# Attention in portions, the second output projection after the last down projection, and a residual added by the stores

## The chip, the cores and the metric

One core of a Trainium2 chip runs the whole program in one launch. The metric is the device time of one execution in microseconds (us). TensorE (PE) multiplies matrices, and PEld are its weight loads. VectorE (DVE) does elementwise work, ScalarE (ACT) copies and activations; GpSimd (POOL) and SyncE (SP) mainly issue DMAs here. Every engine, and every queue of DMA issues, works in its written order: an instruction that waits holds up what is written behind it.

## The reference

The input x has 2048 rows (tokens) of 1024 values, in bf16. What is computed:

```
xn  = layernorm(x)
q, k, v = xn @ wqkv                    # wqkv 1024 x 3072, 32 heads of 32
logits[s, w] = q[s] . k[s - 2 w] / sqrt(32),   w = 0..7, masked below row 0
s   = (softmax over w of logits, times v[s - 2 w], summed over w) @ wo
h   = silu(xn @ w1) * (xn @ w3)        # w1, w3 1024 x 3584
out = x + s * silu(h @ w2)             # w2 3584 x 1024
```

The attention is local and dilated: a token sees eight tokens, itself and every second one before it.

## The kernel before

**Products.** Each large matrix product is done in blocks by a scheme of seven products instead of eight (Strassen's, in Winograd's form). One call of `seven` makes the seven products of one block; each product is eight matmuls of 128x512, in groups named by PSUM tiles (`am`, `em`, `bm` in the MLP, `aq`, `eq`, `bq` in qkv). The operands that are sums of weight quarters are made by VectorE (`qkv_sums`, `w_sums`, `w2_step`), those of the output by adds that read PSUM (`um`, `pk`, `h_sb`) and by copies of ScalarE (`act_copy`, L158) from one PSUM tile to the next, for which TensorE waits. PSUM has four tiles of two banks. The last of the seven products is put off into the next block (`pend`, `flush`).

**Stages, in TensorE's order.** The tokens are handled in two halves b of 1024.

- layernorm and qkv: twelve sevens over q, k, v, two halves, two groups g of heads. Results of the first 512 tokens stay in SBUF; those of the other three quarters are written to DRAM through tiles `pk` (`park`, L334, issued by ScalarE).
- `mlp_up(0)`: 14 blocks `fb` of w1 and w3. In this half VectorE also makes the sums of the weights and of w2 and GpSimd stores them (`s_dram`, `t_dram`), so that the second half only loads them.
- `mlp_down(0)`: seven products of 56 matmuls each, then `wo(0)`: seven products of 16.
- `mlp_up(1)`, `wo(1)`, `mlp_down(1)`, whose `gated` multiplies by the attention's projection, adds x (loaded as `xr`) and stores.

**Attention** is on VectorE, in four chunks c of 512 tokens. `scores(c)` makes, for each of the eight w, one product of 128x4096 and three adds (L405 to L408). `score_sums(c)` sums over the 32 values of a head with eight matmuls on TensorE (tile `zp`, weights `ones`, 128x32 each, to four column strips; L416). `softmax(c)` follows, GpSimd spreads the result out (`Ep`, 16 DMAs a chunk), and `values(c)` makes eight products and eight adds or so of 128x4096 (L444, L456, L457). k, v and q of the next chunk come by `fetch_k` and `fetch_v` on GpSimd's queue.

**Order.** A scheduler places each instruction by priority and the order in which the code is written. Work under `hp()` (high priority) comes first; attention is written under `priority(BG ...)`, far behind, and so fills what the other work leaves. `att_step()` releases the next part of it at seven fixed places. `behind(key)` puts an instruction after a named earlier one (`tc.issue_after`).

**Memory for weights.** `wring` has ten slots; `r4` takes a slot and `release` gives it back. SyncE loads, two blocks ahead. Attention has four tiles (`att`, tag `a8`), small results four more (`kk`, tag `k4`).

Of the kernel before, what the change touches and what calls it, by code (L numbers as in the profile page):

```python
# [17 lines left out]
def kernel(  # L18
# [161 lines left out]
    def seven(key, A, B, e11, e12, e22, e21, snap=None):  # L180
# [21 lines left out]
        act_copy(su2[:], pb[:])  # L202
        for i in I:
            mm(pe[:, i], s4[i], b22, False)
# [3 lines left out]
        e22(pb, sp5)  # L208

# [119 lines left out]
    def park(t, c, j0, name):  # L329
        tl = k4(name, (2, CH), BF16)  # L330
        dst = (q_dram, k_dram, v_dram)[t][c, :, j0:j0 + 2, :]

        def fin():
            m = nc.scalar.dma_start(out=dst, in_=tl[:])  # L334
            if spill:
                d, f = spill.pop(0)
                with tc.issue_after(m.ins):
                    nc.scalar.dma_start(out=d, in_=f)

        return tl[:], fin  # L340
# [6 lines left out]
    def qkv_copy(t, c, j0):  # L347
        def f(ps, *a):
            d, fin = qkv_dst(t, c, j0)
            with hp():  # L350
                if a:
                    nc.vector.tensor_add(d, ps[:], a[0][:])
                else:
                    anchor["c", t, c, j0] = nc.scalar.copy(out=d, in_=ps[:])  # L354
                fin()
        return f
# [29 lines left out]

    def fetch_k(c):
        if c == 0:
            return
        nc.gpsimd.tensor_copy(out=kT[:, :, 0:HALO], in_=kT[:, :, CH:CH + HALO])  # L390
        nc.gpsimd.dma_start(out=kT[:, :, HALO:], in_=k_dram[c])
# [3 lines left out]
    def fetch_v(c):  # L395
        nc.gpsimd.tensor_copy(out=vT[:, :, 0:HALO], in_=vT[:, :, CH:CH + HALO])
        nc.gpsimd.dma_start(out=vT[:, :, HALO:], in_=v_dram[c])

    def scores(c):
        q = qt[c]  # L400
        E = att_tile((W, CH), BF16, f"Es{c}")
        for w in range(W):
            o = HALO - DIL * w
            p_t = att_tile((NJ, CH), BF16, f"pt{c}_{w}")
            nc.vector.tensor_mul(p_t[:], q[:], kT[:, :, o:o + CH])  # L405
            nc.vector.tensor_add(p_t[:, 0:4, :], p_t[:, 0:4, :], p_t[:, 4:8, :])  # L406
            nc.vector.tensor_add(p_t[:, 0:2, :], p_t[:, 0:2, :], p_t[:, 2:4, :])
            nc.vector.tensor_add(E[:, w, :], p_t[:, 0, :], p_t[:, 1, :])  # L408
        sc[c] = E

    def score_sums(c):
        E = sc[c]
        zp = bank2(f"zp{c}")
        for h in range(2):
            for sq in range(4):
                nc.tensor.matmul(  # L416
                    zp[sq * 32:(sq + 1) * 32, h].rearrange("p (w t) -> p w t", t=P), lhsT=ones4[:],
                    rhs=E[:, h * 4:(h + 1) * 4, sq * P:(sq + 1) * P], start=True, stop=True,
                )
        sc[c] = E[:].bitcast(FP32).rearrange("p w n -> p (w n)").rearrange("p (a w t) -> p a w t", a=2, t=P)  # L420
        nc.scalar.copy(out=sc[c][:, 0], in_=zp[:].rearrange("p h (w t) -> p (h w) t", t=P))

    def softmax(c):
        Z = sc[c]
        z, zm, zs = Z[:, 0], Z[:, 1, 0:4], Z[:, 1, 4:8]
# [4 lines left out]
        nc.scalar.activation(out=z, in_=z, func=ACTF.Exp, scale=scale)  # L430
# [8 lines left out]
    def values(c, pairs=(0, 2, 4, 6)):  # L439
        E = pr[c]  # L440

        def pvmul(dst, w):
            o = HALO - DIL * w
            nc.vector.tensor_mul(dst, E[:, w, :].unsqueeze(1).to_broadcast([P, NJ, CH]), vT[:, :, o:o + CH])  # L444

        A = oT[:, c % 2]
        for w0 in pairs:
            B = att_tile((NJ, CH), BF16, f"B{c}_{w0}")
            if w0 == 0:
                pvmul(A, 0)  # L450
                pvmul(B[:], 1)
            else:
                C = att_tile((NJ, CH), BF16, f"C{c}_{w0}")
                pvmul(B[:], w0)
                pvmul(C[:], w0 + 1)
                nc.vector.tensor_add(B[:], B[:], C[:])  # L456
            nc.vector.tensor_add(A, A, B[:])  # L457

    def att_steps():
        with priority(BG - 10000):  # L460
            scores(0)
        yield
        score_sums(0)
        fetch_k(1)
        with priority(BG):
            softmax(0)
            scores(1)
            values(0)
            fetch_v(1)
        yield  # L470
        with priority(BG + 9000):
            fetch_k(2)
        yield
        score_sums(1)
        with priority(BG + 10000):
            softmax(1)
            scores(2)
            values(1)
            fetch_k(3)
            fetch_v(2)  # L480
        yield
        score_sums(2)
        with priority(BG + 20000):
            softmax(2)
        yield
        with priority(BG + 30000), behind("wo"):
            scores(3)
            values(2, (0, 2, 4))
        yield
        score_sums(3)  # L490
        with priority(BG + 40000):
            softmax(3)
            values(2, (6,))
            fetch_v(3)
            values(3)
        yield

    att_it = att_steps()

    def att_step():  # L500
        next(att_it)
# [17 lines left out]
    def up_load(b, fb):  # L519
# [7 lines left out]
        else:  # L527
            up_sums(b, fb, w1t, w3t)
            sa, s4 = tiles[b, fb][2:]
            nc.sync.dma_start(out=sa[:], in_=s_dram[fb, :, 0:2])  # L530
            nc.sync.dma_start(out=s4[:], in_=s_dram[fb, :, 3])
# [3 lines left out]
    def up_sums(b, fb, w1t, w3t):  # L535
        sa = r4(("sa", fb), (2, KH, 2 * P), FP16)
        half.append(half.pop(0))
        s4 = slot(5, (KH, 2 * P), FP16, half[0] * SLOT // 2)
        tiles[b, fb] = w1t, w3t, sa, s4

    def w_sums(fb):
        up_sums(0, fb, *tiles[0, fb])
# [3 lines left out]
        with behind(("m", fb - 1)):  # L546
            nc.vector.tensor_add(sa[:, 0], a21, a22)
            nc.vector.tensor_sub(sa[:, 1], sa[:, 0], a11)
            nc.vector.tensor_sub(s4[:], a12, sa[:, 1])
            nc.vector.tensor_sub(s3, a11, a21)  # L550
# [11 lines left out]
    def mlp_up(b, steps={}):  # L562
        order = [*range(b * FB // 2, FB - 1), *range(b * FB // 2), FB - 1]
        for n, fb in enumerate(order):
            steps.get(n, lambda: None)()
            if n == 0:
                up_load(b, fb)
                if b == 0:
                    w_sums(fb)
                up_load(b, order[1])  # L570
# [8 lines left out]
            def e12(pe, su2):  # L579
# [5 lines left out]
                if b == 0:  # L585
                    anchor["m", fb] = m
                    if fb + 1 < FB:
                        w_sums(fb + 1)
                if n + 2 < FB:
                    up_load(b, order[n + 2])  # L590

            def e22(pb, sp5):
                with hp():
                    m = nc.vector.tensor_add(h_sb[:, f2, CH:], pb[:], sp5[:])  # L594
                if b == 0:
                    anchor["t", fb] = m
                    w2_step(fb)

            def e21(pb, f2=f2, hl=hl, n=n, fb=fb):
                release(("w3", fb))  # L600
                with hp():
                    nc.scalar.copy(out=hl["g"][:, :, 0:CH], in_=pb[:])  # L602
                    nc.vector.tensor_mul(h_sb[:, f2, :], h_sb[:, f2, :], hl["g"][:])  # L603

# [372 lines left out]
```

## Time and profile before

| what | value |
|---|---|
| median of 8 runs | 753.09 us (751.89 to 755.47) |
| the profiled execution | 755.47 us, its span 753.8 us |
| granted TensorE clock, mean | 0.989 |
| PE busy | 724.6 us (96%), 3314 instructions |
| PEld busy | 346.5 us (46%) |
| DVE busy | 619.9 us (82%), 602 instructions |
| ACT busy | 312.8 us (41%) |
| POOL busy | 95.6 us (13%) |
| DMA | 153.68 MB, mean 204 GB/s |
| first product of `first_two` starts | 12.46 us |
| `mlp_up(0)` starts | 169.24 us |
| `mlp_down(0)` starts | 349.70 us |
| `wo(0)` starts | 437.64 us |
| `mlp_up(1)` starts | 461.81 us |
| `wo(1)` starts | 636.70 us |
| `mlp_down(1)` starts | 663.62 us |

A row of the profile names an engine, a line of the kernel, an operation and its output and input tiles; "idle before" is how long the engine had stood still, and the name behind the arrow is what ended that. L148 is the helper `mm`, so TensorE's rows are told apart by the tile names. Matmul ends are modelled: a busy TensorE is not one at its peak, and the distance from start to start of two groups is the safer measure.

### The profile page before, as it was taken

To read this page: it belongs to the slowest core of one execution; us is meant where nothing else is said; L and a number is where in the kernel's file an instruction comes from. 1 tells how busy PE (TensorE), PEld (TensorE's weight loads), DVE (VectorE), ACT (ScalarE), POOL (GpSimd) and SP (SyncE) were. 2 spreads that over 40 slices of the span, in tenths; PEclk is the share of its full clock that TensorE was granted. 3 is DMA by queue.
4 is the path that set the end of the run, shared out by engine and by line. 5 is a ranking of instruction groups with operands and counts; after the bars stand their busy time and mean duration, and the time that the engine had idled before them with its cause. 6 is when DMAs were issued, how large, how long until landed. Compare 5 with 4: busy or idle time off the path is not lost.

```text
span 753.8 us, 8738 instructions
## 1 busy us (share of the span) xinstructions
PE 724.6 (96%) x3314; PEld 346.5 (46%) x3367; DVE 619.9 (82%) x602; ACT 312.8 (41%) x327; POOL 95.6 (13%) x156
## 2 busy tenths in 40 slices
PE   8999999899999999989899999999999999999997
PEld 4655565454444444434344444443444444444443
DVE  8988996879999999999899558999984999552143
ACT  5653345335444555443021443443565454420121
POOL 0000001310212253411001402000032000000000
PEclk9999999899999999999999999999999999999999
DMA  9385449844778799979575989554367543624631
GB/s 332 122 164 178 140 153 311 262 139 165 232 242 268 271 308 297 314 249 333 188 231 180 356 232 287 159 164 128 120 185 230 153 134 118 210 89 135 208 114 56
DMA packets 130218, 153.68 MB, mean 204 GB/s; under 512 B 14976, under 2 KB 100480, under 8 KB 129536
## 3 DMA queue, kind: packets, MB, share of 16 engines
q1 hardware_dynamic: 112960, 102.25, 44.4%
q0 software_dynamic: 11024, 37.76, 14.5%
q10 hardware_dynamic: 6192, 13.11, 4.7%
q8 instruction: 26, 0.43, 0.2%
q14 instruction: 16, 0.13, 0.1%
HBM read 107.48 MB, written 39.32 MB: 195 GB/s over the span
## 4 chain that ended last, share of the span: by engine, by line
PE 48%; DVE 38%; issue 7%; DMA 4%; ACT 2%; SPq 0%; DVEq 0%; ACTq 0%
PE db L148 10%; PE de L148 6%; PE bm L148 6%; DVE pt L405 6%; PE bq L148 5%; PE da L148 5%; PE am L148 4%; PE em L148 3%; DVE pt L406 3%; DVE h_sb L594 3%; PE aq L148 3%; DVE um L581 3%; PE eq L148 2%; DVE B L444 2%; DVE h_sb L603 2%
## 5 line engine op out<-in xcount | busy, mean ns | idle before, releaser
L148 PEld LDWEIGHTS <-wring 128*128 128x128 f16 (+1 forms) x1952 | 205.3, 106 | 233.2 <-issue 21.6
L148 PE MATMUL bm<-xs,wring 128*128 128x512 f16 x672 | 156.8, 380 | 7.4 <-DVE h_sb L594 7.2
L148 PEld LDWEIGHTS <-h_sb 128*128 128x128 f16 (+1 forms) x976 | 103.0, 106 | 120.9 <-issue 12.2
L148 PE MATMUL am<-xT,wring 128*128 128x512 bf16 x424 | 105.6, 382 | 3.1 <-ACT bm L158 1.9
L405 DVE TENSOR_TENSOR pt<-qt,kT 128x4096 bf16<-128x4096 bf16 x32 | 73.1, 2288 | 1.0 <-ACT kT L354 0.5
L148 PE MATMUL db<-wring,h_sb 128*128 128x512 f16 x336 | 73.3, 379 | 0.0
L583 ACT ACTIVATE g<-um 128x1024 bf16<-128x1024 f32 x28 | 29.6, 1057 | 86.3 <-DVE um L581 82.5
L148 PE MATMUL em<-xs,wring 128*128 128x512 f16 x224 | 52.9, 379 | 0.0
L148 PE MATMUL em<-xT,wring 128*128 128x512 bf16 x219 | 52.7, 379 | 0.3
L437 POOL DMA_DIRECT2D Ep<-pb x64 | 36.9, 584 | 125.3 <-DVE pb L433 120.8
L148 PE MATMUL da<-wring,h_sb 128*128 128x512 bf16 x220 | 50.5, 388 | 2.2 <-DMA wring<-in_B_w_dram 2.0
L603 DVE TENSOR_TENSOR h_sb<-h_sb,g 128x2048 bf16<-128x2048 bf16 x28 | 34.1, 1219 | 8.0 <-ACT g L602 8.0
L406 DVE TENSOR_TENSOR pt<-pt 128x2048 bf16<-128x2048 bf16 x32 | 39.0, 1220 | 0.4
L577 ACT ACTIVATE h_sb<-am 128x1024 bf16<-128x1024 f32 x28 | 28.6, 1023 | 21.2 <-PE am L148 21.1
L158 ACT COPY pm<-em 128x1024 f32<-128x1024 f32 x28 | 28.3, 1012 | 21.2 <-PE em L148 21.1
L581 DVE TENSOR_TENSOR um<-em,um 128x1024 f32<-128x1024 f32 x28 | 34.1, 1218 | 3.2 <-PE em L148 3.2
L457 DVE TENSOR_TENSOR oT<-oT,B 128x4096 bf16<-128x4096 bf16 x16 | 36.6, 2285 | 0.1
L158 ACT COPY um<-bm 128x1024 f32<-128x1024 f32 x28 | 28.4, 1014 | 19.9 <-PE bm L148 19.9
L444 DVE TENSOR_TENSOR B<-Ep,vT 128x4096 bf16<-128x4096 bf16 x16 | 36.5, 2284 | 0.0
L602 ACT CAST g<-bm 128x1024 bf16<-128x1024 f32 x28 | 28.3, 1011 | 16.3 <-PE bm L148 15.4
L594 DVE TENSOR_TENSOR h_sb<-bm,pm 128x1024 bf16<-128x1024 f32 x28 | 34.1, 1216 | 0.4 <-PE bm L148 0.4
L158 ACT COPY bm<-am 128x1024 f32<-128x1024 f32 x28 | 28.1, 1002 | 9.9 <-PE am L148 9.8
(180 smaller groups left out, 887.3 us busy)
## 6 DMA issues: line engine op xcount, KB each, us to landing
wring<-in_B_w_dram SPq DMA_DIRECT2D x68, 512.0 KB, 5.4
wring<-t_dram SPq DMA_DIRECT2D x16, 512.0 KB, 4.5
s_dram<-wring POOLq DMA_DIRECT2D x14, 512.0 KB, 3.8
s_dram<-wring POOLq DMA_DIRECT2D x28, 256.0 KB, 5.1
t_dram<-wring POOLq DMA_DIRECT2D x14, 512.0 KB, 6.6
wring<-s_dram SPq DMA_DIRECT2D x28, 256.0 KB, 3.0
wring<-s_dram SPq DMA_DIRECT2D x14, 512.0 KB, 3.7
wring<-in_A_wqkv_dram SPq DMA_DIRECT2D x6, 1024.0 KB, 7.0
```

Of the source, the lines that this page charges most:

```text
L148: nc.tensor.matmul(ps, lhsT=lhs[k], rhs=rhs[k], start=(first and k == 0), stop=(k == n - 1), skip_group_check=not first,)
L158: nc.scalar.copy(out=out_, in_=in_)
L405: nc.vector.tensor_mul(p_t[:], q[:], kT[:, :, o:o + CH])
L406: nc.vector.tensor_add(p_t[:, 0:4, :], p_t[:, 0:4, :], p_t[:, 4:8, :])
L437: nc.gpsimd.dma_start(out=pr[c][r:P:NR, :, sq * P:(sq + 1) * P], in_=pb[sq * 32:(sq + 1) * 32, :, :])
L444: nc.vector.tensor_mul(dst, E[:, w, :].unsqueeze(1).to_broadcast([P, NJ, CH]), vT[:, :, o:o + CH])
L457: nc.vector.tensor_add(A, A, B[:])
L577: nc.scalar.activation(out=h_sb[:, f2, 0:CH], in_=pa[:], func=ACTF.Silu)
L581: m = nc.vector.tensor_add(su2[:], pe[:], su2[:])
L583: nc.scalar.activation(out=hl["g"][:, :, CH:], in_=su2[:], func=ACTF.Silu)
L594: m = nc.vector.tensor_add(h_sb[:, f2, CH:], pb[:], sp5[:])
L603: nc.vector.tensor_mul(h_sb[:, f2, :], h_sb[:, f2, :], hl["g"][:])
```

## The change

1. *Attention in portions.* `att_work` is one generator that yields after each VectorE instruction an estimate of its time. `bg(us)` is called at the end of each `seven` and between the products of `mlp_down`; it takes instructions from the generator until the given sum is used up (`pace["n"]`: 8 per seven in the later qkv, 4.5 in `mlp_up(0)`, 9 in `mlp_up(1)`; a list of quotas in `mlp_down`), and puts them behind the last fixed VectorE instruction (`anchor["v"]`). `drain` empties what must be done before `wo_prepare`.
2. *Score sums* and the exponential get the priority of the place where they are called (`fore`).
3. *Values in halves*: pieces of 128x2048 instead of 128x4096, v fetched in halves. One tile `pt` a chunk instead of one per w.
4. *Weight sums* move to a fixed place in the block (`mid`). The w2 sums are made per `fb` instead of per pair, in pieces of 512 columns. Loads run three blocks ahead.
5. *Queues*: `park` and the spills of x and xs are issued by SyncE instead of ScalarE. The reload of xT and xs stands behind the last load of the down projection.
6. *Order of stages*: `wo(1)` after `mlp_down(1)`. `wo_prepare` makes all sums ahead in both halves, from one load of the upper half of wo.
7. *Residual*: x is copied to `out` in DRAM by seven copies of 512x512 on GpSimd's queue, and the results are added by accumulating stores (14 of 256 KB, GpSimd). The last part is added on VectorE and stored by four plain stores of SyncE.

```diff
     def seven(...):
...
         act_copy(su2[:], pb[:])
+        mid()
...
         e22(pb, sp5)
+        bg(pace["n"])
...
         def fin():                                   # in park
-            m = nc.scalar.dma_start(out=dst, in_=tl[:])
+            m = nc.sync.dma_start(out=dst, in_=tl[:])
             if spill:
                 d, f = spill.pop(0)
                 with tc.issue_after(m.ins):
-                    nc.scalar.dma_start(out=d, in_=f)
+                    nc.sync.dma_start(out=d, in_=f)
...
     def score_sums(c):
-        E = sc[c]
-        zp = bank2(f"zp{c}")
-        for h in range(2):
-            for sq in range(4):
-                nc.tensor.matmul(...)
+        E = sc[c][0]
+        with fore():
+            zp = bank2(f"zp{c}")
+            for h in range(2):
+                for sq in range(4):
+                    nc.tensor.matmul(...)
...
-        nc.scalar.copy(out=sc[c][:, 0], in_=zp[:].rearrange(...))
+            act_copy(sc[c][:, 0], zp[:].rearrange(...))
...
+    def att_work():
+        for c in range(0, NC, 2):
+            yield from scores(c, range(W))
+            fetch_k(c + 1)
+            if c == 2:
+                residual(1)
+            yield STOP
+            score_sums(c)
+            yield STOP
+            exponents(c)
+            yield 3.0
+            yield from scores(c + 1, range(1))
+            weights(c)
+            yield 2.5
+            yield from scores(c + 1, range(1, W))
+            while c == 2 and "wo" not in state:
+                yield STOP
+            v = values(c)
+            for n, t in enumerate(v):
+                yield t
+                if n == 3:
+                    yield STOP
+                    score_sums(c + 1)
+                elif n == 9:
+                    exponents(c + 1)
+                    yield 3.0
+                elif n == 13:
+                    weights(c + 1)
+                    yield 2.5
+            if c == 0:
+                residual(0)
+            yield from values(c + 1)
+            state.add(c + 1)
...
+    def bg(us):
+        if us <= 0:
+            return
+        state_p[0] = tc.cur_priority
+        pace["credit"] += us
+        with priority(BG), behind("v"):
+            while pace["credit"] > 0:
+                t = next(att_it)
+                if t is STOP:
+                    pace["credit"] = min(pace["credit"], 4)
+                    break
+                else:
+                    pace["credit"] -= t
...
     def w_sums(fb):
...
-        with behind(("m", fb - 1)):
-            nc.vector.tensor_add(sa[:, 0], a21, a22)
...
+        nc.vector.tensor_add(sa[:, 0], a21, a22)
...
     # mlp_up
             def e12(pe, su2):
...
-                if b == 0:
-                    anchor["m", fb] = m
-                    if fb + 1 < FB:
-                        w_sums(fb + 1)
-                if n + 2 < FB:
-                    up_load(b, order[n + 2])
+                anchor["v"] = m
+                if b == 1 and n + 2 < FB:
+                    s4_load(order[n + 2])
...
             def e21(pb, f2=f2, hl=hl, n=n, fb=fb):
...
+                if n + 3 < FB:
+                    up_load(b, order[n + 3])
+                if b == 0:
+                    w2_sums(fb - 1)
+                    w2_load(fb)
+
+            def mid():
+                if b == 0 and n + 1 < FB:
+                    w_sums(fb + 1)
...
+    def residual(b):
+        for u, dh in ((0, 0), (1, 1), (0, 1), (1, 0)):
+            if (b, u, dh) != (1, 1, 0):
+                r0 = (2 * b + u) * CH
+                with behind("pool"):
+                    nc.gpsimd.dma_start(out=out_flat[r0:r0 + CH, dh * CH:(dh + 1) * CH], in_=x_flat[r0:r0 + CH, dh * CH:(dh + 1) * CH])
+
+    def finished(b, u, dh, gp, ps, add):
+        last = b == 1 and (u, dh) == (1, 0)
...
+            if last:
+                for i in I:
+                    if gp == 0:
+                        nc.scalar.copy(out=d[:, i], in_=ps[:, i])
+                    nc.vector.tensor_mul(g[:, i], d[:, i] if gp == 0 else ps[:, i], g[:, i])
+                    nc.vector.tensor_add(g[:, i], g[:, i], xw[0][:, gp, i])
+                    nc.sync.dma_start(out=out_rows(out_flat, b, u, dh, gp)[:, i], in_=g[:, i])
+                return
             to_bf16(d, ps, add)
-            anchor["wo"] = nc.vector.tensor_mul(g, d, g)
-            nc.vector.tensor_add(g, g, xw[u, dh][:, gp])
-            nc.gpsimd.dma_start(out=out_rows(out_flat, 0, u, dh, gp), in_=g)
+            anchor["v"] = nc.vector.tensor_mul(g, d, g)
+            nc.gpsimd.dma_start(out=out_rows(out_flat, b, u, dh, gp), in_=g, accum_op=ALU.add)
...
-    mlp_up(0, {1: att_step, 6: att_step})
-    mlp_down(0, mid=lambda n: att_step() if n == 0 else wo_prepare(0))
-    nc.sync.dma_start(out=xT[:], in_=x_dram[:])
-    nc.sync.dma_start(out=xs[:], in_=xs_dram[:])
-    wo(0, finish0)
-    mlp_up(1, {0: att_step, 6: att_step})
-    wo_prepare(1)
-    wo(1, finish1)
-    residual()
-    mlp_down(1, gated)
+    def mid(b):
+        drain(2 * b + 1)
+        wo_prepare(b)
+
+    pace["n"] = 4.5
+    mlp_up(0)
+    mlp_down(0, lambda: mid(0), (7, 10, 10, 9, 9, 3))
+    with behind("dl"):
+        nc.sync.dma_start(out=xT[:], in_=x_dram[:])
+        nc.sync.dma_start(out=xs[:], in_=xs_dram[:])
+    wo(0)
+    state.add("wo")
+    pace["n"] = 9
+    mlp_up(1)
+    mlp_down(1, lambda: mid(1), (7, 10, 10, 9, 9, 3))
+    wo(1)
```

## The prediction

> **What bounds the kernel now.** I read the chain of waits first, to see which engines set the time.
>
> ```profile
> PE 48%; DVE 38%; issue 7%; DMA 4%; ACT 2%; SPq 0%; DVEq 0%; ACTq 0%
> ```
>
> TensorE and VectorE share the end, so neither is the limit everywhere. The windows by stage say where each is (columns: stretch and its length, busy time of PE, PEld, DVE, ACT, POOL, then granted clock).
>
> ```profile
> 141.00:157.00 16.00, 12.84 (x46) 6.44 (x47) 12.50 (x13) 4.97 (x5) 8.54 (x15) 0.79 0.86 271
> 170.00:264.00 94.00, 90.98 (x417) 40.45 (x422) 93.69 (x91) 46.65 (x47) 16.93 (x29) 1.00 0.71 237
> 358.00:437.00 79.00, 76.80 (x352) 34.15 (x354) 65.52 (x44) 16.67 (x16) 13.50 (x21) 0.98 0.73 239
> 460.00:550.00 90.00, 86.74 (x391) 38.34 (x396) 88.47 (x75) 42.89 (x43) 3.56 (x5) 0.98 0.52 160
> 664.00:754.00 90.00, 84.17 (x387) 38.08 (x389) 27.95 (x30) 15.11 (x17) 0.00 (x0) 0.98 0.37 120
> ```
>
> In the first up half (170 to 350) VectorE is full and TensorE waits; in the last down projection VectorE is idle for two thirds. Work could move there. The PE timeline around 141 us shows a single stall, and the one around 123 us the score sums.
>
> ```profile
> 144.11 3.57 PE L148 MATMUL aq<-h_sb 128*128 128x512 bf16 x8 [3.25 <-ACT bq L158]
> 147.48 3.17 PE L148 MATMUL bq<-h_sb,wring 128*128 128x512 f16 x8
> 150.49 1.89 PE L148 MATMUL bq<-h_sb 128*128 128x512 f16 x8
> ...
> 121.00 1.89 PE L148 MATMUL eq<-h_sb,wring 128*128 128x512 bf16 x8
> 122.82 0.62 PE L416 MATMUL zp<-Es,ones 128*32 128x512 bf16 x8
> 123.37 0.44 PE L148 MATMUL aq<-h_sb,wring 128*128 128x512 bf16 x1
> ```
>
> Eight 128x512 matmuls take 1.727 us from start to start (150.49 to 152.21). So an up block of seven such products needs 7 × 1.727 = 12.09 us, and all 406 product groups 701 us. What remains of the span is 12.5 us before the first product, 5.4 after the last, some 4.4 of transposes and score sums, and about 31 us of loss: QKV 11.2, first up half 180.46 − 169.2 = 11.2, second up half 6.9, the rest 2. More than 31 can't be won.
>
> **VectorE's prices** (groups, 128 partitions): 4096 wide 2.285 us, 2048 wide 1.22, 1024 wide 0.685 (bf16) or 1.22 (reading fp32), 512 wide 0.42. An instruction that doesn't need its predecessor's result starts 0.09 early.
>
> **QKV.** At 138.95 VectorE begins the first block's weight sums (`w_sums`, after 1.26 us of wait for their load), then an attention product of 2.28, and only then the add that frees the bank TensorE wants. TensorE's group ahead of the 144.11 row started at 138.97, so 144.11 − 138.97 − 1.73 = 3.41 late, then 3.37 and 3.01 instead of 1.73 each at the lower clock: 6.3 us. In the new written order these sums stand behind the last v add. Two other waits of this kind (1.5 and 0.9 us) should shrink, as 8 us of portions per seven are issued behind its adds. Against it: the 36 stores of q, k, v and 7 of x and xs move from ScalarE's queue (0.33 us of issue each, off the path) to SyncE's, behind weight loads that land in 5.4 us and transposes. A late store holds the next add's tile; I take 0.5 (0 to 3). Sum −6.3 − 2.4 + 0.5 = **−8.2**.
>
> **First up half.** Before, one block holds three 1.22 adds/multiplies, four 0.685 weight sums, half of four 0.685 w2 sums, and attention: 13.54 on average by the written order. It took 12.89, so 0.65 overlaps; 14 × (12.89 − 12.09) = 11.2. After: 3.66 + 2.74 + four 512-wide sums 1.69 + a portion of 4.5 = 12.59, less 0.65 is 11.94, under TensorE's 12.09. But the blocks are uneven. From the new order: 13.4, 13.5, 11.9, 12.7, 12.3, 13.4, 8.1, 15.3, 13.7, 13.3, 13.9, 14.1, 8.2. A block loses what exceeds 12.09 + 0.65 = 12.74, except for about 1.9 us: behind the `um` add stand ScalarE's silu (1.06) and its copy into the next bank (1.00), and from the PE timeline I estimate that TensorE wants that copy 1.9 us after it could be there. The first heavy pair (1.4) is absorbed; the run 15.3 to 14.1 exceeds by 6.6, less 1.9 is 4.7. So the loss falls from 11.2 to 4.7: **−6.5** (−9 to 0).
>
> **Second up half.** 3.66 + 9 = 12.66 per block. The heavy run 13.9, 13.1, 12.9, 12.9, 13.6, 13.6, 13.3, 13.4 exceeds 12.74 by 4.8 and, with the 0.33 overlap this half shows today, 12.42 by 7.5; less 1.9 gives 2.9 to 5.6. I take 3.5, as independent halves of `values` overlap better than score trees: 6.9 → 3.5, **−3.4**. The values of the last chunk move into the last down projection, whose VectorE had 62 us free: 92 us of work by the order in 109 us of products, hidden, unless it piles up before `wo_prepare`. Its removed residual adds (14) and waits there are worth −0.5.
>
> **Score sums.** At foreground priority the order puts them one by one between the matmuls of an `am`/`aq` product (zp, am, zp, am, eight times, four chunks), where they ran together. Eight together cost little because they write four column strips: 122.82 to 123.37 is 0.55, with the 0.09 from 122.73 (121.00 + 1.73) 0.64 in all. Two rounds of 0.216 are 0.43, so a visit there and back costs 0.21 beside. Alone, each costs 0.216 + 0.21: 8 × 0.43 = 3.4, +2.8 per chunk, +11.1 in all. Bounds: without any switch 8 × 0.216 − 0.64 = +1.1, +4.4 in all; with the 0.41 us that the weight loads sit idle on entering this form, +4.4 per chunk, +17.5. I take the row, 11.1, less 2.4 for the one of four that falls in a block where VectorE is late anyway: **+8.7**. The Trainium skill, TensorEngine Tiling (Array Packing), section Key Properties, says that a change of tiling mode drains TensorE, which speaks against this interleaving. It gives no figure; taken as forbidding overlap at every switch, it would put the term nearer the upper bound than the lower one.
>
> **Tail and queues.** Today 748.42 to 753.8 is 5.4 us: silu 0.6, multiply and add 0.85, store. After, the last part ends in copy or multiply, add, and 128 KB stores by SyncE: about 4.7. But the accumulating store of the part before is issued by GpSimd about 0.5 us ahead of TensorE's end, and plain stores of that queue and size take 4.4 to landing; an accumulating one is in no row. I take **+0.5** (−0.7 to +3). The residual copies (7 × 512 KB) replace loads of 4 MB; GpSimd's queue already holds long waits (121 us for `pb`), none of them on the path. xT and xs reload (10.2 and 14.7 us) ahead of wo's w0 load on SyncE: by the order it lands some 5 us before it is wanted, cost 0.
>
> Sum: −8.2 − 6.5 − 3.4 − 0.5 + 8.7 + 0.5 = **−9.4**. The profiled execution took 755.47 (span 753.8 and 1.67 around), the slowest of eight, median 753.09. Span 744.4, that execution 746.1; against the median 753.1 − 9.4 = 743.7. I say **744**.
>
> **Rivals.**
> 1. *The score sums are cheap* (overlapped by the neighbours, or fully beside VectorE's lag): the term 8.7 becomes 0 to 2, so 735 to 737. For it: matmuls of four strips already run beside each other at 122.82. Against: today's 0.21 per visit. 20%.
> 2. *VectorE's lag only moves*: uneven portions and a poor overlap leave both up halves as they are: −9.4 + 9.9 = +0.5, 753.6. For: heavy runs of 15.3 to 13.3. Against: the mean load falls by 0.95 per block. 11%.
> 3. *Slower: SyncE's one queue starves TensorE.* Stores that wait for VectorE now stand ahead of loads, and `w_sums`, now fixed work ahead of the `um` add in VectorE's order, waits for loads. One TensorE idle time over 3 us costs 6.3 us, by the row at 144.11. It decides from 9.4 / 6.3, so from two such stalls: +3.2, 756; three: 762. For: it happened once, with a shorter queue behind it. Against: w3 is issued some 16 us before its sum, and it lands in 5.4. 24%. The Trainium skill, TensorE: Matmul & The Clock Gate, puts the loss of clock at idle windows of about 3.4 us; the case's 3.25 us was already enough, and by the page such a gap would cost its length alone, so that two would not undo the gain.
> 4. *The portions aren't consumed as set* (a backlog drained before `wo_prepare`): each us of backlog is a us of TensorE idle. The written order shows attention finished before; 3%, 750 to 760.
>
> **Chances and range.** The forecast itself (739 to 749) has 42%. A measurement of this kernel can tell about 0.2%, 1.5 us. Faster: 42 + 20 and some of cases 2 and 4, 0.70. Within: most of case 2, 0.05. Slower: case 3, with a slice of 2 and 4, 0.25. The range reaches rival 1's 735 below and 758 above, where two stalls and some lag fit; it leaves out three stalls and score sums at nothing.
>
> **What would show it.** Right: the granted clock at 141 to 157 back at 1.00; up blocks of the first half near 12.1 with some at 12.8 in its second part; the score sums' groups stretched to about 3.4 us per eight; DVE over 75% busy in the last down projection; the last store within 6 us of the last matmul. Wrong: TensorE waits over 2 us on ScalarE copies that wait for VectorE, waits of VectorE on weight loads, or a chain that ends in GpSimd's stores.

## The result, and the profile after

The changed kernel is slower: 760.3 us median against 752.5 of the kernel before, ratio 1.011 (95% interval 1.0091 to 1.0129). Forecast was 744, range 735 to 758. The profiled execution took 759.88 (span 757.8), one of its ordinary ones; that of before, with a span of 753.8, was the slowest of its first eight, so the two traces show only 4.0 of the 8 us.

The chain of waits on the page of the changed kernel:

```profile
PE 57%; DVE 25%; DMA 10%; issue 5%; ACT 2%; SPq 0%; DVEq 0%; POOL 0%; POOLq 0%; ACTq 0%
```

VectorE's share fell from 38 to 25%, and that of DMA rose from 4 to 10%. The windows by stage, for the same stretches as before:

```profile
141.00:157.00 16.00, 15.65 (x64) 8.08 (x65) 5.96 (x7) 6.07 (x6) 1.66 (x3) 1.00 0.90 273
170.00:264.00 94.00, 89.14 (x396) 40.26 (x401) 84.61 (x107) 42.79 (x43) 25.04 (x44) 0.96 0.76 249
358.00:437.00 79.00, 77.66 (x358) 35.19 (x360) 75.37 (x62) 15.01 (x15) 8.21 (x11) 1.00 0.73 252
460.00:550.00 90.00, 89.36 (x403) 39.78 (x409) 59.75 (x57) 45.06 (x45) 10.10 (x10) 1.00 0.66 190
664.00:754.00 90.00, 86.60 (x399) 39.12 (x400) 65.36 (x62) 21.19 (x22) 7.12 (x6) 1.00 0.43 113
```

Three of the five went as forecast: the clock at 141 to 157 is back at 1.00, the second up half keeps TensorE busy, and VectorE has work in the last down projection (65 of these 90 us where it had 28). The first down projection (358 to 437) had no forecast. The first up half went the other way. VectorE, full before (93.69 of 94), now idles for 9 us, 7.3 of them in waits for w2 loads, while TensorE waits too, and the clock is 0.96. Two of the signs of being wrong that the prediction names are here: TensorE waiting over 2 us on a ScalarE copy that waits for VectorE, and VectorE waiting on weight loads. TensorE's timeline there:

```profile
232.55 1.89 PE L148 MATMUL em<-xs,wring 128*128 128x512 f16 x8
238.67 3.57 PE L148 MATMUL am<-xT,wring 128*128 128x512 bf16 x8 [4.23 <-ACT bm L158]
242.04 4.44 PE L148 MATMUL bm<-xs,wring 128*128 128x512 f16 x16
```

And VectorE's, just ahead of the stall:

```profile
234.14 0.42 DVE L672 TENSOR_TENSOR wring<-wring 128x512 f16<-128x512 bf16 x1 [5.32 <-DMA wring<-in_B_w_dram]
```

The `am` group came 238.67 − 232.55 − 1.73 = 4.39 us late; it then took 3.37 instead of 1.73, and the next sixteen matmuls 4.28 instead of 3.45: 6.9 us for one stall. The chain of waits in order of time says why (start, length, what):

```profile
219.79 7.27 DMA t_dram<-wring
227.06 0.02 SPq L575
...
227.58 6.46 DMA wring<-in_B_w_dram
...
234.14 0.43 DVE wring L672
...
235.40 1.23 DVE um L631
...
237.61 1.01 ACT bm L158
...
238.67 3.57 PE am L148 x8
```

SyncE held a w1 load (L575) until a store of w2 sums (`t_dram`) had landed. The w2 load of the current block stood behind it, was issued at 227.58 and landed 6.5 us later. The w2 sums (L672) are fixed work in VectorE's order, ahead of `um`; so VectorE stood still, and `um`, ScalarE's copy and TensorE behind it. SyncE's waits of this kind ahead of w1 loads in the stretch 165 to 375 us (us in total, times, longest), first in the kernel before (L523) and then in the changed one (L575):

```profile
SPq L523 <- DMA t_dram<-wring: 29.8, 5, 8.1
```

```profile
SPq L575 <- DMA t_dram<-wring: 55.6, 9, 11.4
```

Over all loads of that stretch SyncE's waits for these stores were 60.9 us before and are 80.2 now, 14 waits in each. So the path of w2 was slow before too; but VectorE then had no wait for a w2 load in that stretch. In the changed kernel it has:

```profile
DVE wring L672 <- DMA wring<-in_B_w_dram: 15.5, 5, 6.8
```

The score sums are the other visible cost, in TensorE's timeline:

```profile
141.76 0.39 PE L428 MATMUL zp<-Es,ones 128*32 128x512 bf16 x1
142.08 0.44 PE L148 MATMUL aq<-h_sb,wring 128*128 128x512 bf16 x1
142.44 0.39 PE L428 MATMUL zp<-Es,ones 128*32 128x512 bf16 x1
```

A pair takes 0.68 us here and 0.64 in the up blocks, where a product matmul alone takes 0.216.

### The profile page after: what moved, and what is told of

The parts are those of the page before. It is cut to its first block, busy times and chain, and to the rows that moved or that the text cites. A ratio compares the mean times of both kernels' runs of the same rounds, so it can differ in the third digit from the quotient of the medians.

```text
span 757.8 us, 8834 instructions
## 1 busy us (share of the span) xinstructions
PE 730.2 (96%) x3313; PEld 348.8 (46%) x3367; DVE 624.7 (82%) x676; ACT 312.0 (41%) x325; POOL 111.9 (15%) x175
## 4 chain that ended last, share of the span: by engine, by line
PE 57%; DVE 25%; DMA 10%; issue 5%; ACT 2%; SPq 0%; DVEq 0%; POOL 0%; POOLq 0%; ACTq 0%
PE db L148 10%; PE bm L148 7%; PE bq L148 7%; PE de L148 6%; PE am L148 6%; PE da L148 6%; DMA wring<-in_B_w_dram 5%; PE em L148 4%; DVE pt L413 3%; PE eq L148 3%; PE aq L148 2%; DVE um L631 2%; DVE pt L415 2%; PE wb L148 2%; DMA t_dram<-wring 2%
## 5 line engine op out<-in xcount | busy, mean ns | idle before, releaser
L148 PE MATMUL am<-xT,wring 128*128 128x512 bf16 x440 | 110.6, 384 | 7.4 <-ACT bm L158 6.9
L466 DVE TENSOR_TENSOR BC<-Ep,vT 128x2048 bf16<-128x2048 bf16 x56 | 66.8, 1219 | 0.4
L148 PE MATMUL da<-wring,h_sb 128*128 128x512 bf16 x220 | 48.9, 379 | 0.4 <-DMA wring<-in_B_w_dram 0.2
L476 DVE TENSOR_TENSOR oT<-oT,BC 128x2048 bf16<-128x2048 bf16 x32 | 38.9, 1220 | 0.3
L158 ACT COPY pm<-em 128x1024 f32<-128x1024 f32 x28 | 28.3, 1011 | 11.3 <-PE em L148 11.2
L896 POOL DMA_DIRECT2D out_dram<-h_sb x14 | 16.6, 1198 | 105.1 <-DVE h_sb L895 105.1
```

The costliest lines, as they stand in the source:

```text
L148: nc.tensor.matmul(ps, lhsT=lhs[k], rhs=rhs[k], start=(first and k == 0), stop=(k == n - 1), skip_group_check=not first,)
L158: nc.scalar.copy(out=out_, in_=in_)
L476: nc.vector.tensor_add(A, A, B if w0 else C)
```

## The experiments

All are edits of the changed kernel. Steps between them are differences of the ratios to the kernel before, times 752.5 us. "Sums together" is short for the score sums next to each other.

**1. Sums together.**

```diff
                 for sq in range(4):
+                    tc.cur_priority = state_p[0] - 1
                     nc.tensor.matmul(zp[...], ...)
```

> The changed kernel with seven of the eight score-sum matmuls of each chunk next to each other (the first one still has one product matmul behind it); nothing else is meant to move. Theory A, the switches cost TensorE time: in the changed kernel a pair of score sum and product matmul takes 0.64 to 0.69 us, so a chunk costs 3.3 us over its product; together it should cost about 0.64 + 0.25 = 0.9, so -2.4 per chunk and about -9.6 us in all, 750.5. Rival B, VectorE's lag sets the pace anyway and takes the time back as waits of TensorE for ScalarE copies: -3 us or less, 757 or more.

761.3 us, ratio 1.0118 (1.0089 to 1.0147): nothing won. The trace does show the gain (the first up half starts at 165.23 us instead of 167.91), and where it went, in the chain of waits at the start of the down projection:

```profile
362.23 10.58 DMA wring<-in_B_w_dram
...
372.86 1.44 PE da L148 x3
```

TensorE waited 6.46 us for a w2 load, and the granted clock from 357 to 437 us fell to 0.96, where it was 1.00 in the changed kernel. So it was neither theory as stated: in this trace the time was taken by loads, not by VectorE's amount of work.

**2. The w2 load ahead of the w1 and w3 loads on SyncE's queue.**

```diff
+                if b == 0:
+                    w2_sums(fb - 1)
+                    w2_load(fb)
                 if n + 3 < FB:
                     up_load(b, order[n + 3])
-                if b == 0:
-                    w2_sums(fb - 1)
-                    w2_load(fb)
```

> The changed kernel with the w2 load of a block issued ahead of the w1 and w3 loads on SyncE's queue instead of behind the w1 load. Theory A, the queue starves the w2 sums, which are fixed work ahead of the um add: the stall of 4.23 us at 238.67 with the lower clock behind it (6.9 us in all) and the one of 0.38 at 265.86 go, and the waits of the first w2 sum for its load (15.5 us in five) nearly vanish: about -7 us, 753. Rival B, VectorE has too much to do in these blocks and only the place of the wait moves: -1 us or less, 759 or more.

767.1, ratio 1.0198 (1.0169 to 1.0228): slower by 6.6 us. VectorE's waits for w2 loads stayed (15.4 us, now in eight pieces), since the w2 load itself now waited for the store (48.3 us in nine, at L663). The order on the queue alone is not the cause.

**3. Stores of q, k, v, x and xs back on ScalarE's queue.**

```diff
-            m = nc.sync.dma_start(out=dst, in_=tl[:])
+            m = nc.scalar.dma_start(out=dst, in_=tl[:])
...
```

> The changed kernel with the stores of q, k, v and of x and xs back on ScalarE's queue. Theory A, SyncE's queue delays these stores and so VectorE's adds: the waits of the pk adds for stores (6.8 us for v, 0.9 for k) go; the stalls of TensorE near 68.87 and 120.95 (some 5.5 us) shrink: -2 to -5 us, 755 to 758. Rival B, those waits stand where TensorE does not wait for them, and the two stalls come from a weight load and an attention product that VectorE does between the two adds: within 1 us of the changed kernel.

765.4 (760.4 to 770.2), ratio 1.0163 (1.0124 to 1.0201). Undoing this part wins nothing; the spread is too wide to say that it costs. In its trace the waits of the `pk` adds for stores fell from 7.7 to 4.4 us, but the stall near 69 did not shrink (4.13 us of idle, at 72.38).

**4. The last but one part added on VectorE and stored plainly.**

```diff
-                if (b, u, dh) != (1, 1, 0):
+                if (b, u, dh) not in ((1, 1, 0), (1, 0, 1)):
...
+            if plain:
+                nc.vector.tensor_add(g, g, xw[0][:, gp])
+                nc.sync.dma_start(out=out_rows(out_flat, b, u, dh, gp), in_=g)
...
```

> The changed kernel with the last but one part of the last output projection, too, added on VectorE and stored plainly by SyncE; two accumulating stores and one copy of x fewer. Theory A, accumulating stores late on the queue lengthen the end (7.2 us from the end of the last product to the end of the span, where the kernel before had 5.4): -1 to -2 us. Rival B, the end is set by VectorE's chain behind the last product and two more adds of 0.69 lengthen it: 0 to +1 us.

759.7, ratio 1.0092 (1.0059 to 1.0125): not to be told from the changed kernel. In the traces the end shrank a little: 6.6 us from the end of the last product instead of 7.2.

**5. Loads two blocks ahead.**

```diff
-        for fb in order[:3]:
+        for fb in order[:2] if b == 0 else order[:3]:
...
                 anchor["v"] = m                       # in e12
+                if b == 0 and n + 2 < FB:
+                    up_load(b, order[n + 2])
...
-                if n + 3 < FB:                        # in e21
+                if b == 1 and n + 3 < FB:
                     up_load(b, order[n + 3])
```

> The changed kernel with the w1 and w3 loads of the first up half two blocks ahead instead of three, issued beside the um add as before the change. Theory A, three blocks ahead fill the ring (six slots of nine for w1 and w3, two for sums, the rest for w2), so that a load waits for the slot of a w2 store that has not landed, and the loads behind it on SyncE's queue wait too (waits of SyncE for t_dram stores were 55.6 us at L575, 29.8 in the kernel before): the stalls at 238.67 and 265.86 go, -7 us, 753. Rival B, GpSimd's queue (spread of the softmax between the stores) makes the stores late and two blocks ahead suffer as much: within 2 us of the changed kernel. Rival C, the loads come later than the sums want them: slower, 765.

770.4, ratio 1.0221 (1.0191 to 1.0252): slower by 8 us. VectorE waited for w2 loads (12.1 us) and now for w1/w3 loads too (9.9). Two blocks ahead are too few for the sums in this fixed place, so theory A fell in this form, and C held.

**6. The same with the sums together.**

> As e5_two_deep, and the score sums together as in e1_sums_together. There the three chunks outside the stalled stretch gained 2.4 us each in the trace and a stall of 6.6 us on a weight load in the down projection took it back. Theory A (the ring): the loads no longer take it back, so -8 us against e5_two_deep, 745. Rival B, VectorE's lag takes it: -3 us or less against e5_two_deep.

765.8, ratio 1.0170 (1.0140 to 1.0200): −4 us against experiment 5, between the two theories.

**7. That with the next edit and experiment 4's.**

> e6_two_deep_sums with the sums of the v weights behind the adds of the block before (as in e8_v_behind) and the last but one part stored plainly (as in e4_plain). If the parts add up: -8 for the score sums, -7 for the ring, -4 for the v sums, -1 for the end, against 760.3: 740. If VectorE's lag is the bound: 750 or more.

765.5, ratio 1.0174 (1.0142 to 1.0206): the parts don't add up while the loads stall (VectorE waits 11.5 us for w1/w3 loads and 11.0 for w2 loads, and TensorE idles 5.1 us at 243.1).

**8. Sums of the v weights behind the adds.**

```diff
-        qkv_sums(*[wv[i] for i in range(3)])
+        with behind("v"):
+            qkv_sums(*[wv[i] for i in range(3)])
```

> The changed kernel with the sums of the v weights (L315, which waited 1.72 us for its load between the two adds of a block at 66.5 and 70.6) put behind the second add. Theory A: the stall of TensorE of 2.31 us at 68.87 and the lower clock behind it (some 4 us in all) go, -4 us, 756. Rival B: VectorE does the same work later and TensorE waits at the next block: -1 us or less.

757.7, ratio 1.0061 (1.0038 to 1.0084), about 3.7 us won, but not for the reason given: the stall at 68.7 stayed (2.70 us late). Its chain begins in a k store of 7.67 us that holds the tile of the `pk` add. The one at 120.95 (1.62) went.

**9. Two ring slots kept for w2, loads two blocks ahead.**

```diff
+        if fb == 0:
+            t_slots.extend(free.pop(0) for x in I)
-        tiles["t", fb] = r4(("t", fb), (2, 2, CH))
+        tiles["t", fb] = slot(t_slots[fb % 2], (2, 2, CH))
...                                                  # depth as in experiment 5
-        release(("t", fb))
+        if fb == FB - 1:
+            free.extend(t_slots)
```

> The changed kernel with two ring slots kept for the w2 tiles in turn, so that a w2 load waits for the store of two blocks before and no w1 or w3 load waits for a w2 store; w1 and w3 loads two blocks ahead (there is no room for three). Theory A, the loop of w2 load, sums, store and slot is the cause: against e5_two_deep, which has the same depth, the stalls of 5.8 and 4.8 us (with the lower clock some 17) go: -12 us or more, below 758. Rival B, the depth of two is what hurts, as the weight sums wait for loads (9.9 us there): within 3 us of e5_two_deep's 770.

779.2, ratio 1.0353 (1.0322 to 1.0383). Far slower: the depth of two and the w2 loads hurt together (waits of VectorE for w1/w3 loads 17.2 us, for w2 loads 16.6).

**10. That with sums together, v sums behind, plain store.**

> e9_own_slots with the score sums together, the v sums behind and the last but one part stored plainly. Theory A: -9 for the score sums, -3 for the v sums, -1 for the end against e9_own_slots, so about 745. If VectorE's lag is the bound: 755 or more.

771.4, ratio 1.0265 (1.0222 to 1.0308): −6.6 us against experiment 9. The three parts win here too, but less than the loads cost.

**11. No w2 loads and stores in the first up half.**

```diff
-        tiles["t", fb] = r4(("t", fb), (2, 2, CH))
-        nc.sync.dma_start(out=tiles["t", fb], in_=w2_q[:, fb])
...
-        if fb < 0:
+        if fb < 0 or fb > FB - 3:
             return
-        q = tiles["t", fb]
-        b11, b12, b21, b22 = [q[:, x, y] for x in I for y in I]
+        b11, b12, b21, b22 = [xT[:, 0, k] for k in range(4)]
+        o1, o3, o4, o2 = [h16[:, FT - 2 + x, y * CH:(y + 1) * CH] for x in I for y in I]
...
-        nc.gpsimd.dma_start(out=t_dram[:, fb]..., in_=q16)
-        release(("t", fb))
...
```

> The changed kernel without the w2 loads and stores of the first up half: VectorE makes the sums of blocks 0 to 11 from resident data into rows of h not yet written (8 sums of 0.42 us fewer), and the down projections read plain w2 in place of the sums, so their values are others. Theory A (the loop of load, sum, store and slot): the stalls of 4.4 and 0.6 us with the lower clock go, and the wait at the start of the down projection: -9 us against the changed kernel, 751, and with it up blocks near 12.1 but for the one with the score sums. Rival B, VectorE has too much fixed work ahead of um: within 4 us of the changed kernel, as 3.4 us less of sums are no cure.

749.0, ratio 0.9956 (0.9941 to 0.9971): 11.6 us less than the changed kernel. Since the down projections read plain w2 in place of its sums, this kernel and that of experiment 12 compute other values: their times measure the path and are no result to use. VectorE waits for no load in the first up half. SyncE's w1 loads now wait for TensorE alone (L575 among its waits in that stretch):

```profile
SPq L575 <- PE am L148: 105.8, 10, 13.5
```

VectorE is as full as it was before the change (window):

```profile
170.00:264.00 94.00, 91.05 (x416) 41.46 (x422) 93.80 (x134) 46.58 (x46) 24.38 (x43) 1.00 0.62 200
```

No other single edit won as much: the path of w2 through load, sums, store and slot is what costs most. What was left out holds 3.4 us of sums and 28 × 512 KB, some 14 MB, of traffic too, so it does not say which link.

**12. That with the sums together.**

> e11_no_w2 with the score sums together. Theory A: what the score sums gain in the trace (2.4 us a chunk) is not taken back once the loads don't stall: -8 to -10 us against e11_no_w2. Rival B: half or less, -4 us.

740.1, ratio 0.9836 (0.9809 to 0.9864): −9.0 us against experiment 11. TensorE's timeline:

```profile
140.87 0.61 PE L429 MATMUL zp<-Es,ones 128*32 128x512 bf16 x7
141.42 1.95 PE L148 MATMUL aq<-h_sb,wring 128*128 128x512 bf16 x7
```

The seven that stand together take 0.55 us from start to the next group. The interleaving costs its full price once the loads no longer hide it.

**13. The w2 tiles of blocks 0 to 9 in rows of h, in turn.**

```diff
+        if fb < 10:
+            tiles["t", fb] = rows(24 + 2 * (fb % 2), 2).rearrange("p (x y n) -> p x y n", x=2, y=2)
+        else:
             tiles["t", fb] = r4(("t", fb), (2, 2, CH))
```

> The changed kernel with the w2 tiles of blocks 0 to 9 in rows of h that are not yet written (two places in turn) instead of ring slots; everything is computed and stored as in the changed kernel. If the loop through the ring slot is the cause (load of w1 waits for the landing of a w2 store, the next w2 load stands behind it on SyncE's queue, the sums wait for that): the gain of e11_no_w2 less its 3.4 us of sums that are back, -7 to -11 against the changed kernel, 750 to 753. If the gain of e11_no_w2 came from the DMA traffic or the VectorE work that it left out: within 3 us of the changed kernel.

770.6, ratio 1.0230 (1.0205 to 1.0254): slower by 9 us. Freed of the ring, the sums and their loads still wait, now on each other. VectorE's waits, then SyncE's:

```profile
DVE h_sb L675 <- DMA h_sb<-in_B_w_dram: 12.4, 6, 3.9
DVE wring L675 <- DMA wring<-in_B_w_dram: 8.4, 2, 5.6
```

```profile
SPq L666 <- DMA t_dram<-h_sb: 30.9, 7, 8.5
```

So the shared slot alone is not the cause either, and my theory of that time fell.

**14. That with the sums together.**

> e13_w2_in_h with the score sums together. By the step from e11_no_w2 to e12_no_w2_sums (749.0 to 740.1): -9 against e13_w2_in_h, about 742. If VectorE's lag, with its 3.4 us of sums back, takes the gain: -4 or less.

760.7, ratio 1.0105 (1.0079 to 1.0130): −9.4 us. With experiment 12 this puts the price of the interleaving at 9.0 to 9.4 us, in two pairs of kernels.

**15. That with the v sums behind and the plain store.**

> e14_w2_in_h_sums with the sums of the v weights behind the adds (as e8_v_behind, which won 2.6 us) and the last but one part stored plainly (as e4_plain, 0.6). If the parts add up: -3 against e14_w2_in_h_sums, about 739, below both kernels.

758.5, ratio 1.0068 (1.0042 to 1.0095): −2.8 us, as the parts said.

**16. The w2 sums behind the `h_sb` add of the next block.**

```diff
                 anchor["v"] = m                       # in e22
+                if b == 0:
+                    with behind("v"):
+                        w2_sums(fb - 1)
...
-                    w2_sums(fb - 1)                   # in e21
```

> The changed kernel with the four w2 sums of a block put behind the h_sb add of the next block by name, as they stood before the change, instead of where the scheduler's own estimate of the load puts them. Theory A, VectorE meets the sums before their load has landed and um stands behind that wait: the 15.5 us of waits before L672 no longer stand ahead of um, -7 to -9 us, 752. Rival B, the loop through the ring slot alone is too long (sums, landing of the store 6 to 7 us, load behind it 6.5 us, against a block of 12.09): it slips 1 to 2 us a block and the gain is 3 us or less.

782.1, ratio 1.0398 (1.0364 to 1.0432): the slowest of all, against both theories in size. With the ring's slots, VectorE waits longer than ever for w2:

```profile
DVE wring L674 <- DMA wring<-in_B_w_dram: 23.9, 7, 7.1
```

Later sums mean a later store, and SyncE's w2 loads wait for the slots of such stores (43.9 us in nine waits, at L665). That the loop then lasts longer than a block is my reading of these waits; its length was not measured by itself.

**17. That with the tiles in rows of h.**

> e16_sums_behind with the w2 tiles in rows of h as in e13_w2_in_h (770.6). Theory A (place of the sums) with the loop of two blocks: no wait ahead of um in the first up half, -18 against e13_w2_in_h and -8 to -11 against the changed kernel, 750 to 752. If the tiles in h rows are slow for another reason: above 760.

764.3, ratio 1.0142 (1.0116 to 1.0169): −6.6 us against experiment 13 and −19 against 16, so place and slots belong together. But it lies in the range of the rival (above 760) and is no faster than the changed kernel (2.4 us more, not clear of noise). In the first up half VectorE waits for no w2 load any more (4.7 us for w1/w3 loads remain), and from the first up product to the first of the down projection it takes 181.4 us, where the changed kernel takes 184.9 and experiment 11 177.9. So about half of what leaving the path out wins there is won with the path in place. It is more than lost again at the start of the down projection:

```profile
354.08 3.83 PE L148 MATMUL da<-wring,h_sb 128*128 128x512 bf16 x17 [2.55 <-DMA wring<-in_B_w_dram]
...
373.79 13.42 PE L148 MATMUL da<-wring,h_sb 128*128 128x512 bf16 x48 [6.38 <-DVE h_sb L749]
```

The first wait is for a w2 load, the second for the sums of h that VectorE makes for this projection.

**18. That with sums together, v sums behind, plain store.**

> e17_behind_in_h with the score sums together, the v sums behind the adds and the last but one part stored plainly. By the steps measured one by one (-9, -2.6, -0.6) about 739, faster than both kernels by 2%. If VectorE's lag takes it: 748 or more.

751.5, ratio 0.9978 (0.9960 to 0.9997). Faster than the kernel before by 0.2%, about what can be told apart at all, and by 9.9 us than the changed one. The expected 739 was missed at the start of the down projection (TensorE's timeline, then the chain of waits):

```profile
349.91 7.93 PE L148 MATMUL da<-wring,h_sb 128*128 128x512 bf16 x36
363.53 12.48 PE L148 MATMUL da<-wring,h_sb 128*128 128x512 bf16 x48 [5.69 <-DMA wring<-in_B_w_dram]
```

```profile
345.25 1.50 POOL vT L390
...
347.03 0.04 POOLq L682
347.08 0.72 POOL vT L404
347.80 5.83 DMA t_dram<-wring
353.63 0.02 SPq L708
...
353.69 9.71 DMA wring<-in_B_w_dram
```

Attention's copy and fetch of v on GpSimd's queue stand ahead of a w2 store; a w2 load of the down projection waits for that store to land; TensorE waits for that load. It is the same loop at its last turn, and GpSimd's order is one of its links. A version without this was not tried.

## Why the prediction was wrong

Stage by stage, from the starts of TensorE's products in the two profiled executions (us; the last product's end is taken as its start and 16 × 0.216):

| stretch | before | changed | of the difference, score sums | the rest | forecast |
|---|---|---|---|---|---|
| to the first product | 12.46 | 13.37 | | +0.9 | 0 |
| to the third product of `mlp_up(0)` | 162.82 | 161.78 | +3.2 | −4.2 | −8.2 |
| to the last product of `mlp_up(0)` | 177.44 | 185.32 | +2.8 | +5.1 | −6.5 |
| to `wo(0)` | 84.92 | 80.29 | −0.6 | −4.0 | 0 |
| `wo(0)` | 24.17 | 24.17 | | 0 | 0 |
| second up half | 174.89 | 175.21 | +6.2 | −5.9 | −3.4 |
| last down projection and last `wo` | 111.52 | 110.50 | | −1.0 | −0.5 |
| from there to the end | 5.58 | 7.16 | | +1.6 | +0.5 |
| score sums | | | | +11.5 | +8.7 |
| sum | 753.8 | 757.8 | | +4.0 | −9.4 |

(The third product is the mark because the changed kernel puts a qkv product more behind the first one. Of the four chunks of score sums, one that stood in the first down projection, at 389.38, has moved into the second up half.)

- **QKV, forecast −8.2, measured −4.2.** The stall at 144 went as said. The rest was lost to a stall at 68.87 (2.31 us late, and a granted clock of 0.63 and 0.74 over the next two groups, some 4 us in all) and one at 120.95 (1.62). VectorE's add ahead of the first one waited 0.95 us for a k store, a cost that the sum took as 0.5 us for all stores; experiment 8 won a part of this back.
- **First up half, forecast −6.5, measured +5.1: the step that failed.** Its last product starts 7.9 us later after the mark than before, behind the same 28 matmuls of the down projection in both kernels, and 2.8 of that are the score sums. The rows, before and after:

```profile
352.72 1.89 PE L148 MATMUL bm<-xs,wring 128*128 128x512 f16 x8
```

```profile
360.47 1.89 PE L148 MATMUL bm<-xs,wring 128*128 128x512 f16 x8 [1.13 <-DVE h_sb L641]
```

  The sum priced VectorE's work block by block and took it that the w2 sums find their data. With them counted as 1.69 us of work and the wait ahead of them at nothing, the mean of 12.59 meant little: VectorE was idle for 9 of 94 us. Experiment 11, with this path out, ran 11.6 us faster; there the time from the first up product to the start of the last is 183.9 us instead of 192.6.

  The loss that the sum set out to win was too large as well. It measured 180.46 us up to 349.70, where the table of the kernel before has the start of the down projection; TensorE's timeline has that start at 346.68. Up to 349.70 stand 97 of the 98 up products (167.5 us), a qkv product (1.7), 14 matmuls of the down projection (3.0) and a group of score sums (0.6). So the loss was 7.6 us and not 11.2. It became 12.7, where 4.7 was forecast. In experiment 11 it is 4.1, though with 3.4 us less of VectorE's work.
- **First down projection, no forecast, measured −4.0.** Before, TensorE stood 2.01 us at 365.04 for a w2 load, at a granted clock of 0.57 in the 4 us behind; the changed kernel does not wait there. Nothing in the sum foresaw this gain, and without it the forecast would have been 4 us further off.
- **The slower rival named the right kind of cause but not its place.** It spoke of SyncE's queue, waits for loads as fixed work ahead of `um`, and 6.3 us per stall over 3 us. The stall came (6.9 us), but at the w2 sums, not at `w_sums`. I had checked the w1 and w3 loads, issued early enough, and never followed the w2 tile round its loop: load, sums, store, slot, next load. At 24% and 756 us it was given too little of both.
- **Score sums, forecast +8.7.** The four chunks cost 3.8, 3.4, 3.4 and 3.4 us over their products, 11.5 more than before: the row's 11.1 was right and the 2.4 taken off for VectorE's lag was wrong. Pairs of 0.64 to 0.68 give 0.21 to 0.25 us of switching beside the 0.216. This agrees with the Trainium skill, TensorEngine Tiling (Array Packing), section Key Properties, which has each change of mode drain TensorE; the runs show the cost and not the drain itself.
- **Second up half, forecast −3.4.** 175.21 us instead of 174.89 with 6.2 more of score sums: −5.9. Portions did there what they were meant to.
- **Last down projection and tail.** Attention's last values were hidden there, as forecast. The tail was +1.6 instead of +0.5. The plain stores of 128 KB took 3.1 us to landing where they had taken 1.7 before, beside accumulating stores that land in 5.8. In the trace of experiment 4, with the part ahead of them stored plainly too, they took 1.8.

Open stays which link of the w2 path one would have to mend first, and how much of the 11.6 us is its traffic or its 3.4 us of sums. Shown is that leaving the path out wins 11.6 us, and that its slots or the place of its sums changed alone make it worse. Both together end VectorE's waits for w2 in the up half, but TensorE then waits at the down projection's start, and the kernel is no faster than the changed one. How the kernel before keeps its w2 sums cheap (made in pairs, in slots held for two blocks, behind a named add) was not tried as a part by itself.

## What to carry to other kernels

Before pricing an engine's load block by block, follow every tile that goes round a loop of load, work, store and reuse, with the queue of each step: if the loop is longer than the block, or one of its waits stands in fixed order ahead of the add that TensorE needs, the engine's mean load says little. And before pricing what a stage can win, count the products between its two marks: neighbouring stages had lent this one 3.6 us that were no loss. Small matmuls that write other column strips belong next to each other: one by one between full matmuls each cost 0.43 to 0.47 us here, more than five times its share of 0.08 when the eight ran together. And an edit that wins 9 us can show nothing as long as another stall takes it back, so try it again after each cure.

## What the runs showed that was not expected

A stall far below 3 us can lower the clock too. After 2.15 us of idle at 68.87 in the changed kernel the granted clock was 0.63 over the next 3 us, and after 2.01 us of idle at 365.04 in the kernel before it was 0.57 from 365 to 369. After 1.46 us at 120.95 it stayed at 1.00. And stores of the same size and queue landed in 3.1 us instead of 1.7 when they stood behind accumulating stores, and in 1.8 when the part ahead of them was stored plainly (experiment 4); the time of the whole kernel did not show it.
